# Rearranging the fourth attention unit, removing one unread matmul and splitting the last output columns of a fused attention and SwiGLU kernel

## The chip, the cores and the metric

One core of a Trainium2 chip. The metric is the device time of one execution in microseconds (us); lower is better. A profiled execution also has a span, from its first to its last instruction, which is about 2 us shorter than the time.

## The reference

```python
# q, k, v: (4, 8, 768, 64); sort_net: (4, 8, 8, 8); 8 blocks of 96 rows
P = sort_net
for _ in range(5):
    P = exp(P - max(P)); P = P / sum(P, -1); P = P / sum(P, -2)
k_sorted = einsum('bhij,bhjcd->bhicd', P, k_blocks)      # the same for v
attn = softmax(q_block @ k_sorted_block.T / 8)           # block by block
x = (attn @ v_sorted) as (3072, 512)
out = (silu(x @ w_gate) * (x @ w_val)) @ w_out           # d_ff 1536
```

## The kernel before

The work is cut into eight groups of 384 rows. For each group there are four attention units (two heads each): scores, exp, value product, normalisation, transpose into the layout of the feed-forward part. Before the first group there is nothing to overlap its units with, so that stretch, from 17 to 28 us, is ordered by hand. PSUM is the memory that matmuls write here; an eviction, or drain, is the copy from there to SBUF, from which matmuls read. PSUM has eight banks here: pairs `a` and `b`, three that rotate under the tag `gen`, and one called `x`. `fill` is a matmul of zeros whose output nobody reads; it keeps TensorE busy while it waits.

```python
idle_ps = bank_tile("idle_ps", "x")          # the bank x
# ... (cut)
kq_chunk(0, 48, 8, "s", "gen")
fill(idle_ps, 1)
kq_chunk(0, 56, 16, "v", "a")                # mixed keys, drained by VectorE
fill(idle_ps, 1)
kq_chunk(0, 72, 16, "s", "b")                # drained by ScalarE
kq_chunk(0, 88, 8, "v", "gen")
# ... (cut)
fill(idle_ps, 4)
qk(0, 0, "a"); qk(0, 1, "b"); qk(0, 2, "gen")    # scores and exp of units 0, 1, 2
idle_ps = bank_tile("idle_ps")               # from here on a gen bank
fill(idle_ps, 2)
av(0, 0, "a")                                # value product, reciprocal, normalisation
fill(idle_ps, 2)
av(0, 1, "b")
fill(idle_ps, 1)
qk(0, 3, "gen")
av(0, 2, "a")
x01 = xt_tile("x", 2)                        # transposes of units 0 and 1 into bank x
x_to(x01[:, 0], 0, 0); x_to(x01[:, 1], 0, 1)
drain("s", ...)
fill(idle_ps, 1)
av(0, 3, "b")
# ... (cut: transpose of unit 2)
early(0, (0, 1)); early(1, (0, 1))           # gate and value matmuls on units 0 and 1
x3 = xt_tile("x", 1)
x_to(x3[:, 0], 0, 3)
drain("v", ...)
early(0, (2,)); early(1, (2,)); early(2, (0,)); early(0, (3,)) # ... (cut)
```

The weights are loaded by GpSimd in pieces of 256 columns, gate and value in turn, the last ones while the first group runs. The last tile of the output is done in halves:

```python
for part, eng in ((0, "s"), (1, "v")):
    cols = slice(part * DM // 2, (part + 1) * DM // 2)
    o_ps = bank_tile("o_ps")[:, 0:DM // 2]
    # 12 matmuls, then drain(eng, o_sb, o_ps), then a store of these columns
```

The softmax here doesn't subtract the row's maximum and nothing guards it: scores larger than these inputs give would overflow.

## Time and profile before

| | before |
|---|---|
| time, median of the first 3 runs | 250.35 us (249.94 to 250.79) |
| span of the profiled execution | 248.07 us |
| TensorE busy | 97% of the span |
| first score matmul | 20.05 us |
| first gate matmul | 24.82 us |
| first matmul with the last value weights | 42.12 us |
| last store issued, landed | 245.46, 247.16 us |

All positions are counted from the start of the span. A busy share says little here: TensorE is nearly always busy, partly with fills. What counts is which wait ends last at a given point. So one reads the chain of waits for the stretch in question, and then the timeline of the other engines, to see whether what the chain names is a limit or only "the instruction before". The lines are in the prediction below.

### The profile page before, as it was taken

The page shows a single profiled execution, that of the slowest core. Times are in us where ns is not written, and L with a number is a line of the kernel's source. Part 1 is how long each engine was busy: PE and PEld are TensorE (multiplying, and loading weights), DVE is VectorE, ACT ScalarE, POOL GpSimd, SP SyncE. Part 2 cuts the span into 40 slices and gives each one's busy share as a digit, 9 for nine tenths or more (in the row PEclk, how much of TensorE's full clock was granted, in tenths as well). Part 3 has the DMA queues.
Part 4 walks back from the last instruction along what each step waited for, and adds up shares of the span by engine and source line. Part 5 has one row for each costly group of instructions (what it writes and reads, how often), then busy time and mean ns, then how long its engine had stood idle before and what let it go on. Part 6 is the DMA issues. An engine that isn't in the chain of part 4 may idle for free.

```text
span 248.1 us, 6062 instructions
## 1 busy us (share of the span) xinstructions
PE 240.2 (97%) x2572; PEld 142.9 (58%) x2572; DVE 157.4 (63%) x332; ACT 110.3 (44%) x187; POOL 52.6 (21%) x47
## 2 busy tenths in 40 slices
PE   7799999999999999999999999999999999999994
PEld 5385566665555556666655655555555555555543
DVE  6677689886555775857657647755764585446700
ACT  3977543453544444455642552354244334232311
POOL 7948449980039400000000000000000000000000
PEclk9999999999999999999999999999999999999999
DMA  5949999999999488010122121112111111100122
GB/s 97 215 83 162 208 198 223 190 219 222 219 175 188 74 195 179 3 42 3 42 53 56 52 67 32 44 45 74 36 42 42 40 55 55 45 19 24 45 81 88
DMA packets 39530, 24.38 MB, mean 98 GB/s; under 512 B 27728, under 2 KB 35664, under 8 KB 38992
## 3 DMA queue, kind: packets, MB, share of 16 engines
q0 software_dynamic: 21328, 14.16, 39.0%
q1 hardware_dynamic: 18176, 9.84, 14.3%
q8 instruction: 20, 0.33, 0.5%
q14 instruction: 6, 0.05, 0.1%
HBM read 28.32 MB, written 7.86 MB: 146 GB/s over the span
## 4 chain that ended last, share of the span: by engine, by line
PE 88%; DVE 4%; ACT 3%; issue 2%; DMA 2%; DVEq 0%; ACTq 0%; POOLq 0%
PE v_ps L372 24%; PE g_ps L354 23%; PE o_ps L389 23%; PE tkq L233 4%; PE av_ps L303 3%; PE qk L276 3%; DMA v<-in_v_dram 2%; PE idle_ps L415 2%; PE tv L245 2%; PE tv L255 1%; DVE gs_sb L364 1%; PE o_ps L405 1%; DVE st L309 1%; PE x_ps L320 1%; DVE h L377 1%
## 5 line engine op out<-in xcount | busy, mean ns | idle before, releaser
L364 DVE SCALAR_TENSOR_TENSOR gs_sb<-th_sb,g_ps 128x384 bf16<-128x384 bf16 x96 | 52.8, 550 | 53.8 <-ACT th_sb L362 51.2
L372 PE MATMUL v_ps<-xt,wv_sb 128*128 128x384 bf16 x380 | 77.3, 326 | 0.3
L354 PE MATMUL g_ps<-xt,wg_sb 128*128 128x384 bf16 x376 | 76.5, 325 | 0.0
L362 ACT ACTIVATE th_sb<-g_ps 128x384 bf16<-128x384 f32 x96 | 47.1, 491 | 57.6 <-PE g_ps L354 55.2
L389 PE MATMUL o_ps<-wo_sb,h 128*128 128x512 bf16 x276 | 64.3, 379 | 0.0
L377 DVE SCALAR_TENSOR_TENSOR h<-v_ps,gs_sb 128x384 bf16<-128x384 f32 x96 | 53.3, 555 | 6.4
L372 PEld LDWEIGHTS <-wv_sb 128*128 128x128 bf16 x380 | 35.6, 97 | 23.9 <-issue 1.2
L354 PEld LDWEIGHTS <-wg_sb 128*128 128x128 bf16 x376 | 34.5, 97 | 22.9 <-issue 0.2
L389 PEld LDWEIGHTS <-h 128*128 128x128 bf16 x276 | 26.3, 98 | 28.3
L394 ACT COPY o_sb<-o_ps 128x512 f32<-128x512 f32 x23 | 13.5, 586 | 49.1 <-PE o_ps L389 46.4
L124 POOL COPY vch<-v 64x1536 bf16<-64x1536 bf16 (+2 forms) x11 | 28.8, 2648 | 20.6 <-PE av_ps L303 17.2
L289 ACT ACTIVATE e_all<-qk 96x768 bf16<-96x768 f32 x30 | 22.6, 802 | 7.7 <-PE qk L276 7.6
L309 DVE TENSOR_TENSOR st<-av_ps,r_sb 96x512 bf16<-96x512 f32 x32 | 21.7, 679 | 0.2
L303 PEld LDWEIGHTS <-e_all 96*128 96x128 bf16 x256 | 12.2, 98 | 5.0 <-ACT e_all L289 0.8
L303 PE MATMUL av_ps<-vt,e_all 96*128 96x65 bf16 x256 | 13.5, 194 | 0.0
L307 DVE RECIPROCAL r_sb<-av_ps 96x8 f32<-96x8 f32 x32 | 6.4, 199 | 8.7 <-PE av_ps L303 8.6
L213 ACT CAST vt<-tv 96x1024 bf16<-96x1024 f32 (+1 forms) x9 | 9.2, 1030 | 4.0 <-PE tv L255 2.6
L211 DVE CAST vt<-tv 96x1024 bf16<-96x1024 f32 (+1 forms) x9 | 9.8, 1100 | 1.2 <-PE tv L245 1.2
L211 DVE CAST kqt<-tkq 128x1024 bf16<-128x1024 f32 (+1 forms) x7 | 7.4, 1068 | 2.5 <-PE tkq L233 2.4
L213 ACT CAST kqt<-tkq 128x1024 bf16<-128x1024 f32 (+1 forms) x7 | 6.0, 894 | 6.4 <-PE tkq L233 6.4
L415 PE MATMUL idle_ps<-warm_sb 128*128 128x512 bf16 x28 | 8.3, 388 | 0.0
L233 PE MATMUL tkq<-rmix,kq 128*64 128x64 bf16 x384 | 7.8, 197 | 0.4 <-issue 0.4
(74 smaller groups left out, 130.5 us busy)
## 6 DMA issues: line engine op xcount, KB each, us to landing
out_dram<-o_sb SPq DMA_DIRECT2D x23, 256.0 KB, 2.0
v<-in_v_dram POOLq DMA_DIRECT2D x3, 768.0 KB, 19.7
kq<-in_q_dram POOLq DMA_DIRECT2D x2, 768.0 KB, 14.1
wg_sb<-in_moe_w_gate_dram POOLq DMA_DIRECT2D x6, 256.0 KB, 9.4
wv_sb<-in_moe_w_val_dram POOLq DMA_DIRECT2D x6, 256.0 KB, 9.8
wo_sb<-in_moe_w_out_dram POOLq DMA_DIRECT2D x1, 1536.0 KB, 24.5
kp<-in_k_dram POOLq DMA_DIRECT2D x2, 768.0 KB, 15.1
q_scr<-in_q_dram POOLq DMA_DIRECT2D x2, 768.0 KB, 30.0
```

The source lines that it names most:

```text
L124: eng.tensor_copy(dst, src.transpose([0, 2, 1]))
L211: nc.vector.tensor_copy(dst, src)
L233: nc.tensor.matmul(tp[two * D:(two + 1) * D, lc, :], lhsT=kq_tiles[b][:, at + lc, :], rhs=rm[:, two], start=True, stop=True)
L289: nc.scalar.activation(e_all[:, n:n + 2, 0:4 * C], wide[0:C, :, 0:4 * C], AF.Exp, scale=scale)
L303: nc.tensor.matmul(o[:, two, i4, :], lhsT=e[:, i4 * C:i4 * C + 128], rhs=vt[:, 2 * g + two, half * 4 + i4, :], start=True, stop=True)
L309: nc.vector.tensor_tensor(st.rearrange("p i two d -> p two i d"), o[0:C, :, :, 0:D], r_sb.to_broadcast([C, 2, 4, D]), op=ALU.mult)
L354: nc.tensor.matmul(g_ps, lhsT=wg_sb[:, kc, ts(m, 128)], rhs=xt[:, kc, :], start=(kc == 0), stop=(kc == NKC - 1))
L362: nc.scalar.activation(th_sb, g_ps, AF.Tanh, scale=0.5)
L364: nc.vector.scalar_tensor_tensor(gs_sb, th_sb, 1.0, g_ps, op0=ALU.add, op1=ALU.mult)
L372: nc.tensor.matmul(v_ps, lhsT=wv_sb[:, kc, ts(m, 128)], rhs=xt[:, kc, :], start=(kc == 0), stop=(kc == NKC - 1))
L377: nc.vector.scalar_tensor_tensor(h_tiles[n][:, m, :], v_ps, 0.5, gs_tiles.pop(m), op0=ALU.mult, op1=ALU.mult)
L389: nc.tensor.matmul(o_ps, lhsT=h_w[:, m, ts(t3, 128)], rhs=wo_sb[:, m, :], start=(m == 0), stop=(m == NFC - 1))
```

## The change

The intent: ScalarE and TensorE both had gaps in the first four units. The scores of unit 3 begin in the third rotating bank, which only the fills used, so that ScalarE need not pause between the third and the fourth exp. For this the fills stay in bank `x`. Unit 3 is normalised and transposed in halves, so that its second half can go through two engines at once. One unread matmul goes. The last half of the output columns is done in two quarters, so that the last copy and store are shorter.

```diff
+    def scores_half(b, u, two):
+        ps = bank_tile("qk")                 # (cut) four matmuls of one head
     def av(b, u, tag="a", pieces=1):         # (cut)
-        nc.vector.tensor_tensor(st[...], o[0:C, :, :, 0:D], r_sb.to_broadcast(...), op=ALU.mult)
+        n = 4 // pieces
+        for lo in range(0, 4, n):            # the same on n of four blocks
     def out_halves(n, t3):
-        for part, eng in ((0, "s"), (1, "v")):
+        for lo, hi, eng in ((0, DM // 2, "s"), (DM // 2, 3 * DM // 4, "s"), (3 * DM // 4, DM, "v")):
     kq_chunk(0, 56, 16, "v", "a")
-    fill(idle_ps, 1)
     kq_chunk(0, 72, 16, "s", "b")
     qk(0, 2, "gen")
-    idle_ps = bank_tile("idle_ps")
+    qk3 = [scores_half(0, 3, 0)]
     fill(idle_ps, 2)
     av(0, 0, "a")
     fill(idle_ps, 2)
     av(0, 1, "b")
-    fill(idle_ps, 1)
-    qk(0, 3, "gen")
+    qk3.append(scores_half(0, 3, 1))
+    exps(0, 3, None, qk3)
+    fill(idle_ps, 2)
     av(0, 2, "a")
+    fill(idle_ps, 1)
     x01 = xt_tile("x", 2)
     # (cut) transposes and drain of units 0 and 1
-    fill(idle_ps, 1)
-    av(0, 3, "b")
+    av(0, 3, "b", 2)
     # (cut)
-    x3 = xt_tile("x", 1)
-    x_to(x3[:, 0], 0, 3)
-    drain("v", xts[(0, 0)][:, 3:4, :], ...)
-    early(0, (2,))
+    for lo, eng, x3 in ((0, "s", xt_tile("x", 1)), (2, "v", xt_tile("a", 1))):
+        x_to(x3[:, 0], 0, 3, (lo, lo + 1))
+        drain(eng, xts[(0, 0)][:, 3, lo * C:(lo + 2) * C], ...)
+        if lo == 0:
+            early(0, (2,))
```

More of the change, by code (lines that the diff above doesn't have):

```diff
@@ L260 @@
     ecount = [0]
+    def scores_half(b, u, two):
+        half, g = divmod(u, H2)
+        ps = bank_tile("qk")
+        for i4 in range(4):
+            at = (g * NB + half * 4 + i4) * C
+            lo = two * D
+            nc.tensor.matmul(ps[:, i4 * C:(i4 + 1) * C],
+                             lhsT=kqts[b][lo:lo + D, at:at + 128],
+                             rhs=kqts[b][lo:lo + D, GI * C + at:GI * C + at + C],
+                             start=True, stop=True)
+        return ps
     def scores(b, u, tag):
@@ L293, in qk, with av @@
         exps(b, u, *scores(b, u, tag))
-    def av(b, u, tag="a"):
+    def av(b, u, tag="a", pieces=1):
         half, g = divmod(u, H2)
@@ L308, in av @@
         st = ssp.tile([C, 4, 2, D], BF16, name="st", tag="st")
-        nc.vector.tensor_tensor(st.rearrange("p i two d -> p two i d"), o[0:C, :, :, 0:D],
-                                r_sb.to_broadcast([C, 2, 4, D]), op=ALU.mult)
+        n = 4 // pieces
+        for lo in range(0, 4, n):
+            nc.vector.tensor_tensor(st.rearrange("p i two d -> p two i d")[:, :, lo:lo + n], o[0:C, :, lo:lo + n, 0:D],
+                                    r_sb[:, :, lo:lo + n].to_broadcast([C, 2, n, D]), op=ALU.mult)
         sts[(b, u)] = st
@@ L315, in xt_tile, with x_to @@
         return bank[:, 0:n * 4 * C].rearrange("p (g a b) -> p g a b", g=n, b=C)
-    def x_to(dst, b, u):
-        st = sts.pop((b, u))
-        for i4 in range(4):
+    def x_to(dst, b, u, part=range(4)):
+        st = sts[(b, u)]
+        for i4 in part:
             nc.tensor.transpose(dst[:, i4, :], st[:, i4].rearrange("p a b -> p (a b)"),
@@ L400, in out_halves @@
         base = b * S + half * TW + t3 * 128
-        for part, eng in ((0, "s"), (1, "v")):
-            cols = slice(part * DM // 2, (part + 1) * DM // 2)
-            o_ps = bank_tile("o_ps")[:, 0:DM // 2]
+        for lo, hi, eng in ((0, DM // 2, "s"), (DM // 2, 3 * DM // 4, "s"), (3 * DM // 4, DM, "v")):
+            cols = slice(lo, hi)
+            o_ps = bank_tile("o_ps")[:, 0:hi - lo]
             for m in range(NFC):
@@ L406, in out_halves @@
                                  start=(m == 0), stop=(m == NFC - 1))
-            o_sb = opool.tile([128, DM // 2], FP32, name="oh_sb", tag="oh_sb")
+            o_sb = opool.tile([128, DM // 2], FP32, name="oh_sb", tag="oh_sb")[:, 0:hi - lo]
             drain(eng, o_sb, o_ps)
@@ L475 @@
     av(0, 1, "b")
+    qk3.append(scores_half(0, 3, 1))
+    exps(0, 3, None, qk3)
+    xts[(0, 0)] = xtp.tile([128, H2, TW], BF16, name="xt0_0", tag="xt")
+    fill(idle_ps, 2)
+    av(0, 2, "a")
     fill(idle_ps, 1)
-    xts[(0, 0)] = xtp.tile([128, H2, TW], BF16, name="xt0_0", tag="xt")
-    qk(0, 3, "gen")
-    av(0, 2, "a")
     x01 = xt_tile("x", 2)
@@ L500 @@
     early(1, (0, 1))
-    x3 = xt_tile("x", 1)
-    x_to(x3[:, 0], 0, 3)
-    drain("v", xts[(0, 0)][:, 3:4, :], x3.rearrange("p g a b -> p g (a b)"))
-    early(0, (2,))
+    for lo, eng, x3 in ((0, "s", xt_tile("x", 1)), (2, "v", xt_tile("a", 1))):
+        x_to(x3[:, 0], 0, 3, (lo, lo + 1))
+        drain(eng, xts[(0, 0)][:, 3, lo * C:(lo + 2) * C], x3[:, 0, lo:lo + 2].rearrange("p a b -> p (a b)"))
+        if lo == 0:
+            early(0, (2,))
     early(1, (2,))
```

## The prediction

> **What bounds the kernel now.** I read the page first (shares, then the chain that ended last), then the chain and the timeline of the two stretches that the change touches, then the waits of TensorE.
>
> ```profile
> PE 240.2 (97%) x2572; PEld 142.9 (58%) x2572; DVE 157.4 (63%) x332; ACT 110.3 (44%) x187; POOL 52.6 (21%) x47
> ...
> PE 88%; DVE 4%; ACT 3%; issue 2%; DMA 2%; DVEq 0%; ACTq 0%; POOLq 0%
> ```
>
> TensorE carries 88% of the chain; after 42 us its work is dense and the change does not touch it until the last tile. So only three places can move the end: the chain before the feed-forward part (17 to 28 us), whatever carries that stretch's end forward, and the tail after 242 us. First the chain of 17 to 28 us (start, length, what):
>
> ```profile
> 17.95 0.32 PE idle_ps L415
> 18.27 0.88 PE tkq L233 x48
> 19.15 0.97 PE idle_ps L415 x4
> 20.12 0.62 PE qk L276 x24
> 20.74 0.54 PE idle_ps L415 x2
> ```
>
> It calls warm-up matmuls (L415, output never read) critical, but the chain only says "the instruction before on its engine". The timeline of the other engines shows the real limits:
>
> ```profile
> 17.99 1.89 DVE L211 CAST kqt<-tkq 128x1024 bf16<-128x1024 f32 x2 [0.79 <-PE tkq L233]
> 18.94 1.01 ACT L213 CAST kqt<-tkq 128x1024 bf16<-128x1024 f32 x1 [1.48 <-PE tkq L233]
> ...
> 22.00 0.69 DVE L309 TENSOR_TENSOR st<-av_ps,r_sb 96x512 bf16<-96x512 f32 x1
> 22.84 0.69 DVE L309 TENSOR_TENSOR st<-av_ps,r_sb 96x512 bf16<-96x512 f32 x1
> 23.72 0.69 DVE L309 TENSOR_TENSOR st<-av_ps,r_sb 96x512 bf16<-96x512 f32 x1
> 23.96 1.36 ACT L213 COPY xt<-x_ps 128x768 bf16<-128x768 bf16 x2
> 24.68 0.69 DVE L309 TENSOR_TENSOR st<-av_ps,r_sb 96x512 bf16<-96x512 f32 x1
> 25.84 0.36 DVE L211 COPY xt<-x_ps 128x384 bf16<-128x384 bf16 x1 [0.47 <-PE x_ps L320]
> ```
>
> See two things. The two evictions of the mixed keys on VectorE run without a gap until 17.99+1.89 = 19.88, those of ScalarE until 19.95. And from 21.77 (first reciprocal, 0.20 each) to 25.37 VectorE does four units of reciprocal plus normalisation back to back: 3.6 us for four times 0.92. That stretch is VectorE's, not TensorE's.
>
> TensorE's weight loads then show an absolute deadline:
>
> ```profile
> 42.02 0.36 PEld L372 LDWEIGHTS <-wv_sb 128*128 128x128 bf16 x3 [0.27 <-DMA wv_sb<-in_moe_w_val_dram]
> ```
>
> This is the first use of the last piece of the value weights. The transfer was issued at 28.85 and took 13.1 us to land (41.97). Its time does not depend on TensorE. The tail:
>
> ```profile
> 243.69 0.37 ACT L213 COPY oh_sb<-o_ps 128x256 f32<-128x256 f32 x1 [0.68 <-PE o_ps L405]
> 244.09 1.70 SPq L409 DMA_DIRECT2D out_dram<-oh_sb  x2
> 245.00 0.42 DVE L211 COPY oh_sb<-o_ps 128x256 f32<-128x256 f32 x1 [9.33 <-PE o_ps L405]
> ...
> out_dram<-o_sb SPq DMA_DIRECT2D x23, 256.0 KB, 2.0
> out_dram<-oh_sb SPq DMA_DIRECT2D x2, 128.0 KB, 1.7
> ```
>
> Last matmul ends 244.95, VectorE copies 245.00 to 245.42, the store is issued 245.46, lands 1.70 later (247.16), and the program closes at 248.1.
>
> **What the Trainium skill says.** (1) "TensorE: Matmul & The Clock Gate", Back-to-back issue gap: N/2.4 + 2.5 ns between matmul starts when warm. The trace agrees: starts are 216 ns apart at N=512, 162 at 384, 42.5 at 96. I use the rule for N=128, which no row here has: 56 ns, an estimate. (2) Same page, Part 3, The mechanism: loads overlap running matmuls when the row group differs. The score matmuls of before alternate two row groups and start in pairs (3 ns apart, one pair per 42.5 ns); the new half-score function keeps one row group, so I count 42.5 ns each with no pairing. (3) "DMA: Bandwidth & Descriptors", Specifications: at least 512 B for line rate; Anatomy of one DMA: a fixed cost of about 2 us, mostly the write receipt, plus bytes over 436 per ns. The slope agrees: 2.0 for 256 KB and 1.7 for 128 KB is 0.3 us per 128 KB; the fixed part here is smaller, about 1.4. Quarter rows are exactly 512 B, so still at line rate. (4) "PSUM — Partial Sum Buffer", bank collisions: engines must be kept apart by bank; that is why the two halves of the fourth transpose go to two banks, one read by ScalarE, one by VectorE. No run shows a collision.
>
> **The change part by part.**
>
> *Unread matmul removed.* At 17.884; the next mixing matmul starts 18.204, so 0.32 us leaves TensorE (0.216 plus a tile-shape switch of about 0.10, seen whenever TensorE goes between 128-column and 64-wide work). ScalarE's eviction starts 0.32 earlier and ends at 19.63. But VectorE's still ends at 19.885: its first starts at 17.99, from matmuls ahead of the removed one. The scores need both. First score matmul: 20.054 before; after, 19.885 plus 0.06 to 0.10 for the semaphore = about 19.99. Gain s = 0.06, not 0.32.
>
> *Scores of unit 3 in the spare bank.* Four matmuls at 42.5 = 0.17 go before the two fills. TensorE is ready for the first value product 1.23 after the first score; the exp ends 1.19 after it, plus 0.055: 1.25. No loss. ScalarE now runs the fourth exps straight after the third (22.70 instead of 23.09), so they end at about 23.45, not 23.96. But ScalarE's next work, the transposes of units 0 and 1 (23.965), waits for TensorE, whose order is now: second half of the scores 22.38 to 22.56; switch 0.09; two fills 0.44; third value product at 23.10 (23.01 before); fill; transposes of unit 0 from 23.58, of unit 1 from 23.75, done 24.08. All minus s. So that eviction starts at about 24.05 instead of 23.965: 0.09 later. The earlier exp buys nothing, because VectorE was the bound.
>
> *Normalisation in halves.* VectorE's 512 elements take 0.687: by its slope (384 in 0.55, 512 in 0.687, about 1.05 ns per element) 0.15 is fixed. Halves take 0.42 each, 0.15 more in all. Unit 3's reciprocal starts 24.52-s; halves end at 25.18-s and 25.63-s (25.37 before).
>
> *Transposes in halves.* TensorE starts the first gate matmuls at 24.97-s = 24.91 (24.815 before); four at 0.162, half a, the gate's third, half b end at 25.95-s. The drains of 192 columns: ScalarE 0.32 (0.48 at 384, 0.80 at 768), VectorE 0.26. Half b is in SBUF at about 26.4-s = 26.35 against 26.19 before. But the order view of the changed kernel shows the first value matmul of the second block hoisted ahead of the first that needs unit 3, so the 0.12 that TensorE waited at 26.13 is filled. Sum to the end of this block: +0.09 (late start) - 0.12 (wait filled) + 0.02 = 0.0, give or take 0.1.
>
> *And the deadline.* Even a gain of 0.1 to 0.3 here meets the weights at 41.97: TensorE sits there 0.27 before the load. In before, VectorE's release of the bank (42.06) and the weights come together, so a gain is swallowed, while a loss passes through. I book 0.0 to +0.05.
>
> *Last columns in quarters.* TensorE: 24 matmuls of 256 at 0.109 become 12 of 256 and 24 of 128 at 0.056: +0.03. The last ends at 244.99. The final copy is 128 columns: 0.425 is 0.16 + 256 x 1.04, so 0.29: it ends at 245.31. Its store is half as large: 1.70 - 0.15 = 1.55. Landing 245.35 + 1.55 = 246.90 instead of 247.16: -0.26. The third quarter's store is issued at about 244.66 and takes 0.33 of the queue, so it is clear of the last.
>
> Sum: -0.26 (tail) + 0.03 (front) = -0.23 us of 250.35.
>
> **The rivals.** (a) The front gain is real and reaches the end: the author removes 0.32 of TensorE and 0.39 of ScalarE's idle time, and 0.12 of waiting. For it: the chain names those pieces. Against it: VectorE's unbroken run and the weights at 41.97. If the weights land earlier in runs without the profiler, up to 0.3 more: 249.8. (b) The front loses: two normalisations, late transposes and more fills make the gate matmuls 0.1 to 0.2 late, and VectorE's chain carries it through: 250.3. For it: VectorE has no slack there. (c) The tail gives nothing: the receipt, not the bytes, sets the last store, so only the 0.13 of the shorter copy stays, or a third store in flight delays the last: 250.2 to 250.4. For it: 1.4 of the 1.7 us is fixed.
>
> **Range and chances.** The runs of before spread 0.85 us (249.94 to 250.79), more than the effect. I predict 250.1, with 249.6 to 250.6 holding it 8 times in 10. Two per cent is 5 us; nothing touched can be worth that unless something breaks: 0.98 within 2%, 0.01 on either side.
>
> **What would show it.** Right: first score matmul at 19.95 to 20.0, with TensorE idle ahead of it; VectorE unbroken from the first reciprocal to the second half; ScalarE idle ahead of the first transposes' eviction; the wait at 26.1 gone; the weight load at about 42.0 with as long a wait or longer on the transfer; last copy 0.29 long, last landing about 1.55 after its issue. Wrong: the load of the last value weights earlier than 41.8 or waiting for no transfer, a first score before 19.85, or a last landing over 1.65.

## The result

| | before | changed |
|---|---|---|
| time, median of 4 runs | 250.51 us (249.94 to 250.79) | 250.31 us (250.12 to 250.81) |
| ratio, 95% interval | | 0.9998 (0.9974 to 1.0022) |
| span of the profiled execution | 248.07 us | 248.37 us |

A ratio here is the mean time of one kernel's runs over that of the other's of the same rounds, so it is not quite the ratio of the medians. The change is worth nothing that the runs can resolve: the interval is 0.65 us down to 0.55 us up. The two profiled executions differ by +0.29 us, and this much the traces account for. The page of the changed kernel, shares and chain:

```profile
PE 239.7 (97%) x2584; PEld 143.2 (58%) x2584; DVE 157.4 (63%) x333; ACT 110.6 (45%) x189; POOL 52.6 (21%) x47
...
PE 87%; DVE 6%; ACT 3%; issue 2%; DMA 1%; DVEq 0%; ACTq 0%
```

VectorE has 6% of the chain instead of 4%. Of the 4.7 us more, only 1.83 are from the change: its eviction of the mixed keys, ahead of which the chain no longer goes through a fill. The rest lies before 6 us, where the chain goes through VectorE's part of the softmax instead of a load. The chain of 17 to 28 us shows the first, and one thing more (start, length, what):

```profile
17.94 1.83 DVE kqt L211 x2
19.77 0.14 issue
19.91 0.69 PE qk L288 x24
...
22.55 0.54 PE idle_ps L429 x2
23.09 0.26 PE av_ps L315 x8
23.35 0.23 PE idle_ps L429
23.58 0.04 issue
23.62 0.51 PE x_ps L334 x8
24.14 0.02 issue
24.16 0.81 ACT xt L213
24.97 0.04 issue
25.01 0.48 PE g_ps L510 x2
```

The first score matmul now waits for VectorE's eviction, as predicted. But from 23.35 to 23.62 the chain goes through a fill, and here it is a true limit: the transposes begin 0.04 after the fill has *ended*, not when TensorE could issue them. And the eviction of the transposes (24.16) is 0.20 later than before (23.96), although everything ahead of it is earlier. The timeline says who was idle meanwhile, and what became of the halves:

```profile
24.16 1.18 ACT L213 COPY xt<-x_ps 128x768 bf16<-128x768 bf16 x2 [0.84 <-PE x_ps L334]
24.66 0.75 DVE L323 TENSOR_TENSOR st<-av_ps,r_sb 96x256 bf16<-96x256 f32 x2
25.95 0.32 ACT L213 COPY xt<-x_ps 128x192 bf16<-128x192 bf16 x1 [0.60 <-PE x_ps L334]
26.20 0.26 DVE L211 COPY xt<-x_ps 128x192 bf16<-128x192 bf16 x1 [0.79 <-PE x_ps L334]
```

ScalarE has won 0.84 us of idle time and waits for TensorE. VectorE, too, stands idle for 0.11 us ahead of the last unit's reciprocal (at 24.31): in this stretch it is no longer unbroken. The drains of the halves cost what was predicted (0.32 and 0.26); the two normalisations cost less, 0.07 more than the whole one and not 0.15, because they overlap (0.75 for two). The last value weights, in the timeline of weight loads:

```profile
42.15 0.16 PEld L386 LDWEIGHTS <-wv_sb 128*128 128x128 bf16 x2 [0.30 <-DMA wv_sb<-in_moe_w_val_dram]
```

As before, TensorE's weight load comes just after the landing (42.11 in this execution). And the tail, in the timeline and in the list of transfers:

```profile
243.82 0.37 ACT L213 COPY oh_sb<-o_ps 128x256 f32<-128x256 f32 x1 [0.68 <-PE o_ps L419]
244.22 1.59 SPq L423 DMA_DIRECT2D out_dram<-oh_sb  x3
245.16 0.29 DVE L211 COPY oh_sb<-o_ps 128x128 f32<-128x128 f32 x1 [9.36 <-PE o_ps L419]
...
out_dram<-oh_sb SPq DMA_DIRECT2D x1, 128.0 KB, 1.7
out_dram<-oh_sb SPq DMA_DIRECT2D x2, 64.0 KB, 1.6
```

The final copy takes 0.29 instead of 0.42, and the last store lands 1.56 after its issue, at 247.03: earlier than before (247.16), although the tail began 0.12 later. So the quarters did what they were to do. Yet the span ends 0.29 later. What is left is the stretch after the last landing: 0.92 us before, 1.33 now. It holds waits of SyncE for the completion semaphores of the transfers, one after the other, and then the program's last steps, which take 0.9 us in both. From the trace's records (start of each wait's instruction, in us):

```text
before:  last landing 247.16
  245.84 245.91 245.97 246.04 246.10 246.16 246.22 246.28 | 247.17            end 248.07
changed: last landing 247.03
  245.86 | 247.05 247.12 247.18 247.24 247.30 247.36 247.42 247.48            end 248.37
```

Each wait takes 0.06. Before, eight of nine are over before the last landing and one comes after it. Now one is over and eight come after. Seven more times 0.06 is 0.43.

The accounts of the profiled pair: the matmul with the last value weights is 0.10 later; from there to ScalarE's copy of the first half 201.60 us instead of 201.58 (+0.02); from that copy to the last landing 3.22 instead of 3.46 (-0.25); from there to the end +0.42. The sum is +0.29.

### The profile page after: what moved, and what is told of

It reads as the page before. It is cut to its first block, busy times and chain, and to the rows that moved or that the text cites. A ratio compares the mean times of both kernels' runs of the same rounds, so it can differ in the third digit from the quotient of the medians.

```text
span 248.4 us, 6091 instructions
## 1 busy us (share of the span) xinstructions
PE 239.7 (97%) x2584; PEld 143.2 (58%) x2584; DVE 157.4 (63%) x333; ACT 110.6 (45%) x189; POOL 52.6 (21%) x47
## 3 DMA queue, kind: packets, MB, share of 16 engines
q0 software_dynamic: 21328, 14.16, 39.1%
## 4 chain that ended last, share of the span: by engine, by line
PE 87%; DVE 6%; ACT 3%; issue 2%; DMA 1%; DVEq 0%; ACTq 0%
PE v_ps L386 24%; PE g_ps L368 23%; PE o_ps L403 23%; PE tkq L233 4%; PE av_ps L315 3%; PE qk L288 2%; PE tv L245 2%; PE tv L255 1%; DVE gs_sb L378 1%; PE idle_ps L429 1%; PE o_ps L419 1%; DVE st L323 1%; PE x_ps L334 1%; DVE h L391 1%; DVE kqt L211 1%
## 5 line engine op out<-in xcount | busy, mean ns | idle before, releaser
L323 DVE TENSOR_TENSOR st<-av_ps,r_sb 96x512 bf16<-96x512 f32 (+1 forms) x33 | 21.8, 663 | 0.2
L233 PEld LDWEIGHTS <-kq 128*64 128x64 bf16 x384 | 6.7, 113 | 1.9 <-issue 1.6
```

Of the source, the lines that this page charges most:

```text
L233: nc.tensor.matmul(tp[two * D:(two + 1) * D, lc, :], lhsT=kq_tiles[b][:, at + lc, :], rhs=rm[:, two], start=True, stop=True)
L323: nc.vector.tensor_tensor(st.rearrange("p i two d -> p two i d")[:, :, lo:lo + n], o[0:C, :, lo:lo + n, 0:D], r_sb[:, :, lo:lo + n].to_bro ...
```

## The experiments

The table holds what all profiled executions showed, before any single one is discussed. "From first score" are positions counted from the first score matmul, because the first score itself lies between 19.40 and 20.05 mostly for reasons that the edits do not touch: TensorE begins to mix the keys at 14.16 to 14.56 us, and in ten of the fourteen executions it pauses near 17 us (see what is left open). From the start of the mixing to the first score it is 5.12 to 5.24 us without that pause and 5.34 to 5.76 with it. When the last of the first keys land (15.8 to 16.7 us) does not decide it: e3_slot and e12_tail2 have them at 15.84, and their first scores at 19.40 and 19.98. "Release" is the end of VectorE's instruction that frees the bank which the matmul of the last value weights needs; "landing" is that of the weights. All in us.

| kernel | from first score: transposes | first gate | fifth unit | landing | release | matmul | copy to last landing | last landing to end |
|---|---|---|---|---|---|---|---|---|
| before | 3.23 | 4.76 | 7.75 | 41.97 | 42.06 | 42.12 | 3.46 | 0.92 |
| changed | 3.72 | 5.10 | 7.99 | 42.11 | 42.16 | 42.22 | 3.22 | 1.33 |
| e1_bank | 3.50 | 4.89 | 7.78 | 41.66 | 41.76 | 41.81 | 3.22 | 1.33 |
| e2_tail | 3.23 | 4.76 | 7.75 | 44.42 | 42.60 | 44.46 | 3.21 | 1.34 |
| e3_slot | 3.23 | 4.76 | 7.74 | 42.20 | 41.41 | 42.25 | 3.46 | 1.35 |
| e4_front | 3.72 | 5.10 | 7.99 | 42.12 | 42.10 | 42.17 | 3.47 | 0.90 |
| e5_joined | 3.72 | 5.10 | 8.00 | 41.74 | 41.88 | 41.93 | 3.23 | 0.92 |
| e7_nofill | 3.28 | 4.76 | 7.65 | 41.77 | 41.70 | 41.82 | 3.22 | 1.33 |
| e8_split | 3.71 | 5.10 | 7.99 | 40.29 | 41.89 | 41.94 | 3.33 | 1.34 |
| e9_all | 3.28 | 4.76 | 7.65 | 44.07 | 42.53 | 44.12 | 3.33 | 0.90 |
| e10_two | 3.28 | 4.76 | 7.65 | 41.02 | 41.59 | 41.64 | 3.23 | 0.90 |
| e11_move | 3.28 | 4.76 | 7.65 | 40.33 | 41.72 | 41.92 | 3.33 | 0.90 |
| e12_tail2 | 3.23 | 4.76 | 7.75 | 40.95 | 41.99 | 42.04 | 3.23 | 0.92 |
| e13_whole | 3.28 | 4.76 | 7.75 | 41.99 | 41.49 | 42.03 | 3.22 | 1.35 |

(For e8_split, e9_all and e11_move the landing is that of the first of two pieces.)

Two things make it readable. The stretches repeat to 0.01 or 0.02 us between executions, so one profile is enough for them. And the matmul of the last value weights starts 0.05 after the later of landing and release, in all but e11_move. From it to the last score matmul of the kernel it is 155.66 us, give or take 0.04, in ten of the eleven kernels that change nothing in between; the other is e10_two.

The timed runs (5 rounds, except e13_whole with 1) are weaker. Some executions of before and of most other kernels take 251.5 to 253.7 us (none of changed, e4_front, e5_joined, e7_nofill and e13_whole did). Two profiles fell on such executions (e2_tail and e9_all), and both show the weights landing at 44.1 to 44.4; e11_move is that slow for another reason, given below. What makes the weights late there is not known, and it widens the intervals to half a per cent.

**e1_bank: the fill in another bank.** The first theory: the transposes write bank `x`, the fill ahead of them writes it too, so they wait for its end.

```diff
     av(0, 2, "a")
-    fill(idle_ps, 1)
+    fill(bank_tile("idle_ps"), 1)
```

> Changed kernel with one edit: the single fill ahead of the first transposes writes a bank of the rotating three instead of the bank that the transposes write. Counted from the first score matmul, the changed kernel starts the transposes of unit 0 at 3.72 us and the first gate matmul at 5.10. Theory A (the transposes wait for the end of the fill because both write one bank): transposes at 3.50, ScalarE's first transpose eviction 0.2 earlier, first gate matmul at 4.90. Rival B (the split normalisation and the two fills ahead of the third value product are what is late): nothing moves, 3.72 and 5.10. On the end: if the landing of the last value weights is a deadline (42.0 to 42.1), the first matmul with them stays at 42.1 or so and the 0.2 is lost there; if not, the matmul comes at 42.0 and the span is 0.2 shorter than the changed kernel's.

Measured: 3.50 and 4.89, as theory A says. The chain:

```profile
22.90 0.26 PE av_ps L315 x8
23.16 0.22 PE idle_ps L429
23.37 0.36 PE x_ps L334 x8
23.73 0.02 issue
23.75 0.81 ACT xt L213
24.56 0.04 issue
24.60 0.48 PE g_ps L510 x2
```

From the start of the fill to the first transpose it is 0.22 us, the issue of its 512 columns; in the changed kernel it is 0.44. Theory A is shown, rival B is not. Here landing and release were both early (41.66 and 41.76), so nothing was lost at the weights, but this execution also had its first score 0.19 earlier, since TensorE began to mix the keys 0.24 earlier. Time 250.24 us against 250.10, ratio 1.0006 (0.9954 to 1.0058): not resolved.

**e2_tail: the quarters alone.** The kernel before with the new last tile.

```diff
-        for part, eng in ((0, "s"), (1, "v")):
+        for lo, hi, eng in ((0, DM // 2, "s"), (DM // 2, 3 * DM // 4, "s"), (3 * DM // 4, DM, "v")):
```

> Kernel before with the quarters of the last columns alone. Counted from ScalarE's copy of the first half, the last store lands at 3.47 us before and 3.21 in the changed kernel; from that landing to the end of the span it is 0.88 before and 1.31 in the changed kernel. Theory D (closing waits: the third store takes the completion semaphore that is waited for first, so seven more waits run after the last landing): 3.21 and 1.31, span 0.17 longer than before. Rival E (a third store in flight makes the receipt or the program's end later by itself): 3.21 and 1.31 too; the next run tells D from E. If the quarters are a gain as predicted: 3.21 and 0.88, span 0.26 shorter.

Measured: 3.21 and 1.34. The profiled execution was one with late weights, in the timeline of weight loads:

```profile
44.46 0.11 PEld L372 LDWEIGHTS <-wv_sb 128*128 128x128 bf16 x2 [1.88 <-DMA wv_sb<-in_moe_w_val_dram]
```

so its span (250.60) is not to be compared; the two stretches of the tail are. Time 250.03 against 250.10, ratio 1.0005 (0.9954 to 1.0057).

**e3_slot: only the place of the semaphore.** The traces show that the transfers on this queue take one of eight completion semaphores in turn. In the kernel before the last store has the eighth, with the third store of the change it has the first. One small load that nobody reads shifts the turn and leaves the tail alone.

```diff
+    spare = const.tile([BH, NB, NB], FP32)
+    nc.sync.dma_start(out=spare, in_=sn)
     merge(ffn(4), units(2, range(4, 8), (0.0, 8.0)))
```

> Kernel before with one more small load of 8 KB on the same queue, far from the end, never read; the last columns stay in halves and only two stores are in flight at the end. It shifts the last store from the eighth completion semaphore to the first. Theory D: landing 3.47 us after ScalarE's copy as before, but 1.31 from landing to the end instead of 0.88, span 0.43 longer. Rival E: 3.47 and 0.88, no change.

Measured: 3.46 and 1.35. Same stores, same landing, 0.43 more after it. Theory D is shown, rival E is not. Time 250.51 against 250.10, ratio 1.0019 (0.9966 to 1.0072).

This execution shows the deadline as well. It lacks the pause near 17 us, its first score came 0.65 before that of the kernel before, and yet the matmul of the last value weights came 0.13 later:

```profile
42.24 0.11 PEld L372 LDWEIGHTS <-wv_sb 128*128 128x128 bf16 x2 [1.16 <-DMA wv_sb<-in_moe_w_val_dram]
```

VectorE's release was at 41.41; TensorE's weight load sat there 1.16 us. A lead of 0.65 us was lost whole.

**e4_front: the front alone.** The changed kernel with the halves of before in the last tile.

```diff
-        for lo, hi, eng in ((0, DM // 2, "s"), (DM // 2, 3 * DM // 4, "s"), (3 * DM // 4, DM, "v")):
+        for part, eng in ((0, "s"), (1, "v")):
```

> Changed kernel with the halves of the kernel before in the last columns, so the front part alone. First gate matmul 5.10 us after the first score; from there on everything 0.1 later than in before; 3.47 and 0.88 at the end; span 0.1 longer than before (less or more by the jitter of the first loads, 0.1 to 0.2). If the front is a gain: span shorter than before.

Measured: 5.10, 3.47, 0.90, span +0.06. Time 250.13 against 250.10, ratio 0.9989 (0.9948 to 1.0030).

**e5_joined: quarters in two stores.** The half and the first quarter are stored together, so the last store has the eighth semaphore again.

```diff
             drain(eng, o_sb[:, lo:hi], o_ps)
-            nc.sync.dma_start(out=out[ds(base, 128), cols], in_=o_sb)
+            if lo:
+                first_col = 0 if eng == "s" else lo
+                nc.sync.dma_start(out=out[ds(base, 128), first_col:hi], in_=o_sb[:, first_col:hi])
```

> Changed kernel with the last columns still computed and copied as a half and two quarters, but stored in two stores (384 columns, then 128), so the last store is again on the eighth completion semaphore. Theory D: the last store still lands 3.21 us after ScalarE's copy of the half starts, and the end comes 0.90 after the landing (1.33 in the changed kernel). Span 0.43 shorter than the changed kernel at the same start of the last value weights' matmul. If it is the number of stores in flight or the small size that holds the end back: 1.33 stays.

Measured: 3.23 and 0.92. The last store is still small and still quick, in the list of transfers:

```profile
out_dram<-oj_sb SPq DMA_DIRECT2D x1, 192.0 KB, 1.9
out_dram<-oj_sb SPq DMA_DIRECT2D x1, 64.0 KB, 1.6
```

With e3_slot this settles it from both sides. Time 249.78 against 250.30, ratio 0.9991 (0.9958 to 1.0024).

**e7_nofill: no fill ahead of the transposes.**

```diff
     av(0, 2, "a")
-    fill(idle_ps, 1)
     x01 = xt_tile("x", 2)
```

> Changed kernel without the single fill ahead of the first transposes. Theory A goes further: transposes of unit 0 start at 3.28 us after the first score, those of unit 1 wait for VectorE's second normalisation (3.53), first gate matmul at 4.75, the fifth unit's scores at 7.64 after the first score (7.99 in the changed kernel, 7.78 with the fill in another bank, 7.75 before). If TensorE's warm clock needed that fill, the granted clock drops below 0.99 and the matmuls lengthen. Matmul of the last value weights: at the later of VectorE's release plus 0.05 and the landing plus 0.05, so part or all of the 0.35 may be lost there.

Measured: 3.28, 4.76, 7.65, clock 1.0. The chain up to the gate matmuls is now VectorE's:

```profile
22.57 0.69 DVE st L323
23.26 0.01 issue
23.26 0.21 DVE r_sb L319
23.48 0.02 issue
23.50 0.70 DVE st L323
24.20 0.05 issue
24.25 0.34 PE x_ps L334 x4
```

That is the bound that the prediction named; it binds only once the fill is gone. The first gate matmul stands where it stood before the change, and the fifth unit 0.10 earlier than before. Part was lost at the weights: release 41.70, landing 41.77. Time 250.02 against 250.30, ratio 0.9985 (0.9959 to 1.0011).

**e8_split: last value weights in two pieces.**

```diff
-    for m in range(1024, DF, 256):
-        load_gv(m, m + 256)
+    load_gv(1024, 1280)
+    load_w(wg_sb, wg_dram, 1280, DF)
+    load_w(wv_sb, wv_dram, 1280, 1408)
+    load_w(wv_sb, wv_dram, 1408, DF)
```

> Changed kernel with the last load of value weights cut into two of 128 columns, so that the first matmul needs only the first. If that landing is the deadline that swallows gains of the front: first half lands near 41.0 instead of 42.1, the load of the weights no longer waits for a transfer, and the matmul starts 0.05 after VectorE's release, whatever the run's jitter. In this kernel VectorE and the landing come together, so little time is won: 0 to 0.1. Rival: the pieces of 128 columns move slower and the second half or the next key load lands later by over 1 us; then the time is the same or worse.

The first piece landed at 40.29, and the matmul came 0.05 after VectorE's release: the deadline was gone. But the kernel got slower, 251.18 against 250.30, ratio 1.0035 (1.0008 to 1.0063), and not by slow pieces. TensorE waited in another place, in the timeline of weight loads:

```profile
48.26 0.23 PEld L247 LDWEIGHTS <-vch 128*128 128x128 bf16 x6 [1.13 <-POOL vch L124]
```

GpSimd issues these loads in order, and with one more of them it stood idle for 2.66 us, until the value blocks had landed (35.62), before it issued the load of the output weights: at 35.90 instead of 32.33 in the changed kernel. GpSimd's four copies of value blocks come behind it and began at 36.99 instead of 35.53, and the value mixing of the second batch waits for those copies.

**e9_all: no fill, two stores, two pieces.**

> The three together: no fill ahead of the transposes, two stores, last value weights in two pieces. If the three causes are the right ones they add: fifth unit's scores 7.64 us after the first score, last value weights' matmul at VectorE's release plus 0.05 (about 41.8 where the first score is at 19.9), 3.21 and 0.90 at the end: span 0.35 + 0.43 = 0.8 shorter than the changed kernel and 0.5 shorter than before, time about 249.6. If a later deadline (the value blocks of the second batch copied by GpSimd until 47.07) takes its place, 0.1 to 0.3 of it is lost.

Front and tail added up as expected (3.28, 4.76, 0.90). The time did not follow: 250.96 against 250.30, ratio 1.0029 (0.9996 to 1.0062). The profile fell on an execution with late weights, so the first piece too landed only at 44.07, and the wait for GpSimd's copies was there again (0.5 us). A miss; the profile shows the reason of e8_split once more, but how much of the time each of the two delays took is not shown.

**e10_two: no fill and two stores.** The edits of e7_nofill and e5_joined.

> Changed kernel without the fill ahead of the first transposes and with two stores in the last columns; weight loads as they are. Front as measured without the fill: transposes 3.28 us and first gate matmul 4.76 after the first score. End: last landing 3.22 after ScalarE's copy starts, 0.91 from there to the end. If the two causes add: time 0.4 to 0.6 below before and 0.4 to 0.7 below the changed kernel, less what the landing of the last value weights swallows. If they do not add: like the two-store run alone, 0.2 to 0.5 below before.

Measured: 3.28, 4.76, 3.23, 0.90; span 247.67, 0.41 below before and 0.70 below the changed kernel. The weights landed early (41.02), so the matmul came at the release, 41.64. Then 0.28 was lost: TensorE waited at 47.3 for GpSimd's copies, which end when the value blocks' landing (35.1 to 36.0 where the weights are not late) and four copies of 2.8 us say. Time 249.86 against 250.08, ratio 0.9990 (0.9956 to 1.0024): the lowest median but that of e5_joined, not clear of noise.

**e11_move: with the output weights loaded after the copies.** As e10_two, plus the two pieces, plus:

```diff
-    nc.gpsimd.dma_start(out=wo_sb, in_=wo_dram)
     # (cut)
     for s in range(4):
         copy_v(nc.gpsimd, 0, highr, s)
+    nc.gpsimd.dma_start(out=wo_sb, in_=wo_dram)
```

> The same, plus the last value weights in two pieces, with the load of the output weights moved behind GpSimd's four copies of value blocks, so that it does not hold those copies back. The reason given for the loss of the kernels with two pieces (the value-mixing matmuls waited 0.9 us at 48.3 for GpSimd's copies) says: that wait is gone or under 0.1; output weights land near 56, before their first use at 58; the matmul of the last value weights starts 0.05 after VectorE's release. Time as without the pieces or up to 0.2 better. If instead smaller pieces cost time by themselves, it stays near 251.

The matmuls no longer waited for GpSimd's copies, as expected. The matmul of the last value weights came 0.20 after VectorE's release and not 0.05: TensorE had stood idle for 0.32 us until 38.87, for the piece of value weights before, and so was itself the last to be ready. And the output weights, issued at 47.18, landed at 59.47 and not near 56, and their first user waited, in the timeline of weight loads:

```profile
59.51 0.55 PEld L404 LDWEIGHTS <-h 128*128 128x128 bf16 x4 [1.86 <-DMA wo_sb<-in_moe_w_out_dram]
```

Time 251.90 against 250.08, ratio 1.0079 (1.0038 to 1.0119). My expectations of the landing and of the matmul at 42 us were wrong. With the wait of 42 us removed, the one of 48 binds, and with that removed, one at 59: three transfers in a row have almost no slack.

**e12_tail2: the two-store quarters on the kernel before.**

> Kernel before with quarters of the last columns in two stores, front untouched. Theory D: landing 3.22 us after ScalarE's copy starts (3.46 before), 0.91 from landing to the end (0.92 before): span 0.25 shorter from that copy on, the predicted gain of the quarters without the closing waits. If a third store or the small store costs by itself: less than 0.1.

Measured: 3.23 and 0.92: 0.23 less than before from the copy on. Time 249.98 against 250.08, ratio 1.0021 (0.9974 to 1.0069), with two executions above 252 in it.

**e13_whole: e7_nofill with unit 3 whole again.**

> Changed kernel without the fill ahead of the first transposes, and with the fourth unit's normalisation, transposes and drain whole, as before. From the first gate matmul to the fifth unit's scores it is 2.99 us before and 2.89 with the halves. If the halves give the 0.10: 2.99 here, with the wait of 0.12 for the drain back. If the order of the score matmuls gives it: 2.89.

From the first gate matmul to the fifth unit 2.99 us, as before; with the halves it is 2.89. So the halves give the 0.10 and the order of the scores does not. One round only.

## Why the prediction was right or wrong

The predicted 250.1 with 249.6 to 250.6 held, and "within 2%" too. That is in part luck: the range also holds no change at all (250.35), and the loss of 0.32 us that the traces give below would have lain outside it (250.67), had it not been lost in the scatter of the runs. The parts were not all right; two errors went the same way.

*First score.* Right. The unread matmul gave little, because VectorE's eviction is the limit. Counted from the start of VectorE's first long eviction of the second half of the keys, the first score comes at 2.06 in the four profiled kernels with the fill (before, e2_tail, e3_slot, e12_tail2) and at 1.97 in the ten without: a gain of 0.09, predicted 0.06. (It came at 19.91, outside the 19.95 to 20.0 that was named as a sign of being right, because the eviction itself began 0.05 earlier.)

*Scores in the spare bank.* Right: the first value product starts 1.245 after the first score (1.247 before).

*Transposes.* Wrong in one term, the one that reads "fill; transposes of unit 0 from 23.58". I let the transposes follow the fill after its issue time. They follow its end, because both write bank `x`. Keeping the fills in that bank, to free the rotating one, is what the change itself does. The predicted loss from first score to first gate matmul was 0.16 (24.97 against a first score of 20.05, both without the gain s, less the 4.76 of before); measured 0.34. e1_bank gives back 0.21 by moving only the fill's bank. The Trainium skill, "PSUM — Partial Sum Buffer", Engine vs sequencer instructions, says that matmuls start and complete in program order; by this alone two matmuls on one bank would need no wait. But the program has one: in the trace the first transpose waits for a semaphore that only TensorE's own instructions raise. I had the program's listing before predicting and did not look for waits of an engine on itself. So the premise "that stretch is VectorE's" did not hold in the changed kernel: VectorE stood idle there for 0.11 us, and the fill was the limit.

*Halves.* Right: 0.10 gained, shown by e13_whole. One term in it was too large: the split normalisation costs 0.07 more and not 0.15. (Also, the four times 0.92 us of VectorE in the prediction are four times 0.90.)

*Sum of the front.* Predicted 0.0, give or take 0.1. Measured -0.09 + 0.34 - 0.10 = +0.15, and 0.05 of it was covered by chance, as VectorE's eviction began 0.05 earlier in the changed kernel's execution. Rival (b), a loss in the front that is carried through, is what happened: the first gate matmul came 0.20 late, and of the causes named there it was a fill, though by its bank and not by its number; VectorE's chain did not carry it.

*Deadline.* Right that a gain there can be lost: shown in e3_slot, e7_nofill and e13_whole (release 41.49, landing 41.99), and that a loss passes through. What I had not seen is that the landing moves by executions from 41.0 to over 44; it came 1.8 and 1.5 us after VectorE's release in the two slowest profiled executions. That it makes most of the scatter of the time is likely, but not shown: each kernel was profiled once.

*Quarters.* Landing right to 0.01: 3.22 from the copy for a predicted 3.21 (246.90 less 243.69), a store of 1.56 for a predicted 1.55. Wrong is the last term, unspoken: that the end follows the landing at a fixed distance. The sum "-0.26 (tail)" should have been -0.25 + 0.42 = +0.17. Rival (c), that a third store delays the last, is excluded for the transfer itself by e2_tail (3.21); it is right only in that the third store moves the semaphore.

So the balance: +0.15 in the front and +0.17 in the tail, where -0.23 was predicted. The timed runs cannot tell these apart, since executions of one kernel spread over 0.7 us and more. That they show 0.9998 is no proof that the changed kernel is not 0.2 slower.

Left open: in before, changed and eight others TensorE pauses for 0.2 to 0.5 us near 17 us without any wait that the profile shows, in e2_tail, e3_slot, e11_move and e13_whole it does not; and the last store took 1.66 instead of 1.56 in the three kernels with the weights in two pieces.

## What to carry to other kernels

A warm-up matmul ahead of work that is ready costs its issue (0.22 us, e7_nofill against e1_bank), and if the next real matmul writes the same bank, in this program the wait for its end too (0.21 more); look in the listing for waits of an engine on itself. Count to the end of the program and not to the last landing: splitting the last store may put more closing waits after it. And before shortening a stretch that runs beside loads, look how long the next first use of loaded data already waits; if landing and compute come together, the gain needs an earlier load first.

## What the Trainium skill lacked or had wrong

- "PSUM — Partial Sum Buffer", Engine vs sequencer instructions: that matmuls complete in order does not mean that a program reuses a bank on TensorE freely. Here the program waits for the end of the earlier matmul, which cost 0.21 us against another bank (e1_bank).
- No page that I read has the closing waits: the program waits for the eight completion semaphores of a queue in a fixed order at the end, 0.06 us each; the place of the last store among them is worth up to 0.43 us (0.92 against 1.35 after the landing, e3_slot).
- "TensorE: Matmul & The Clock Gate", Back-to-back issue gap: the sustained figures there, about 81 ns at N=128 and 131 ns at N=512 with a weight load per matmul, were not found; the trace has 56 ns and 216 ns with a weight load each, which is the page's formula.
- "DMA: Bandwidth & Descriptors", Anatomy of one DMA: its fixed 2.0 us is for transfers issued by GpSimd; the stores issued by SyncE took 1.56 us for 64 KB, 1.70 for 128 KB and 2.0 for 256 KB.
- "TensorEngine Tiling (Array Packing)", Key Properties, says that a change of the tiling mode drains TensorE but gives no figure: each step between matmuls of 64 rows and of 128 rows cost 0.09 to 0.11 us here.
